# An attention and expert kernel: first expert weights asked for later, unread matmuls in free banks, transfers counted for each queue

## The chip, the core and the metric

The kernel runs on one core of one Trainium2 chip. The core has five engines that each run their own list of instructions in order: TensorE (PE, matrix multiplies, with its weight loads shown apart as PEld), VectorE (DVE), ScalarE (ACT), GpSimd (POOL) and SyncE (SP, which here only issues DMA transfers). They wait for each other through semaphores. The metric is the time of one execution in microseconds (us), taken on the device.

## The reference

The input is attention over 8 batches of 8 heads, 576 positions, 64 wide; the first four heads see a window of the last 32 positions, the other four every fourth of the last 128. Its output, 4608 rows of 512, goes through a layer of eight experts, of which each row takes the one with the highest logit:

```python
scores = scale * np.matmul(q, k.transpose(0, 1, 3, 2))
...
scores = np.where(masks[None, :, :, :], scores, -1000000000.0)
...
attn = attn / (np.sum(attn, axis=-1, keepdims=True) + 1e-09)
return np.matmul(attn, v).astype(np.float32)
...
logits = x @ w_gate
expert_idx = np.argmax(logits, axis=1)
...
for e in range(E):
    lo, hi = (boundaries[e], boundaries[e + 1])
    h = np.maximum(x_sorted[lo:hi] @ w1[e], 0.0)
    y_sorted[lo:hi] = h @ w2[e]
y = y_sorted[inv_perm]
return (gate_w[:, None] * y).astype(np.float32)
```

Everything is fp32: w1 is 512 x 1024 and w2 1024 x 512 for each expert, 2 MB each.

## The kernel before

**The stages.** Attention is cut into 16 pairs (a batch and one of the two kinds of heads), each in two units. A unit goes: `scores` on PE (L602), mask on DVE (L618), exp on ACT (L636), sums and reciprocals on DVE, scaling on POOL (L653), transposes of the scaled weights on PE into a bank called `weights` (L664), their eviction from that bank by ACT or DVE (`eT`, L894), and the product with `v` on PE (`xo`, L692). After both pairs of a batch are done, PE computes the gate's logits and the ranks of the rows within their experts, POOL scatters the rows of that batch into a table in DRAM (`bucket`), and tables say which expert owns which 128 rows.

The experts' work has four parts. Eight single slots of 128 rows run between the attention units as soon as a batch fills them (`ph`, L1525, is the first product, `py`, L1541, the second); the weights of the first two are asked for early, as eight transfers of 1 MB (L522). Then come ten pairs of slots: two slots' products share fourteen smaller ones, for which DVE adds up blocks of the two experts' weights and rows (L1819), PE multiplies (L1925 and L1932), and DVE puts the results together (L2055). Between the pairs run fourteen blocks of 32 rows (`ph_s`, L1635, and `py_s`) for what is left of an expert. Five slots close the kernel. Results are scattered to the output by POOL (L1566).

**What sets the order.** Nothing of this order is written out by hand. Each step is given to `Plan` with an estimated duration, a rank, the buffers that it takes and uses and the steps that it comes after (`after`). `Plan.write` then plays the kernel through with these estimates: it keeps the time at which each engine is free, picks the step that could start soonest, of those within 0.25 us the one with the lowest rank, and writes it out. Each engine then executes its steps in the order written. An `after` that no data and no buffer stands behind is thus only a place in the order; in the kernel itself there is no wait for it. For transfers the plan keeps a time until which the DMA engines move data (`moving`), to which each transfer adds its `moved`.

**Queues.** SP issues `q` and `k` (both into `raw`, L386), `v` (L412, L419, L436), the first weights (L522), the weights (L1511) and rows `x` (L1482) of single slots, the rows of 32-row blocks (`own`, L1588), and the pairs' rows `xp` (L1482) and weights (L1790, two buffers for w1 and two for w2, in turn). Each of SP's transfers also waits for the one eight places ahead of it. POOL issues the scatters and, on its own queue, the weights of 32-row blocks (L1623): w1 as two transfers into `raw`, w2 as one into `raw` and two into `qT`.

**Unread matmuls.** Where the plan sees PE idle, or its clock low, it writes small matmuls whose result nobody reads (L732), ahead of the step that PE would idle for. The plan's count is `max(min(MOST, int(idle / us)), WARMING if cold else 0)`. They write to the last quarter of the bank that `weights` or `rank` last took (`spare[0]`), so they come behind whatever still reads that bank. They end with the first matmul of the first single slot.

Of the kernel before, what the change touches and what calls it, by code (L numbers as in the profile page):

```python
# [33 lines left out]
CAP = N  # L34
# [15 lines left out]
NSLOT = SINGLES + max(E, MOST_SLOTS - FIRSTS - 2 * PAIRS)  # L50
TAIL = SINGLES + 5
# [22 lines left out]
MOVED_S = 1.5  # L74
# [47 lines left out]
class Plan:  # L122
# [19 lines left out]
    APART = 0.21 * IDLE  # L142

# [67 lines left out]
    def write(self):  # L211
# [8 lines left out]
        while open_:  # L220
# [114 lines left out]
def kernel(  # L335
# [222 lines left out]
    def turn_pe(p, n, m):  # L558

        tp = bank("turned", 6, 64)  # L560
# [99 lines left out]
    def weights(ev, g):  # L660
        tp = bank("weights", 4, 128)
        spare[0] = tp[:, 3]
# [61 lines left out]
    def hold(name):  # L724
        return Hold(ring[name])
# [3 lines left out]
    spare = [bank("unread", 4, 128)[:, 3]]  # L729

    def fill():
        nc.tensor.matmul(spare[0], lhsT=idle, rhs=idle, start=True, stop=True)  # L732
# [19 lines left out]
    def attention():  # L752
# [12 lines left out]
        for p, (b, ty) in enumerate(pairs):  # L765
# [40 lines left out]
            )  # L806
            hq, hk = hold("qT"), hold("kT")
            turned[p] = []
            for n in range(2 if p < BY_PE else 0):
                for m in range(3):  # L810
                    hb, T = hold("misc"), {}
# [27 lines left out]
            quad = p < QUADS  # L839
            for hp in range(2):  # L840
# [3 lines left out]
                if hp == 0 or not quad:  # L844
# [4 lines left out]
                    def score(e, i=i, units_of=units_of, tags=tags):  # L849
# [4 lines left out]
                        "PE", 1.76 if p < BY_PE else 3.35 if quad else 1.7 if p < WHOLE else 0.88, score,  # L854
# [76 lines left out]
    def route(b, hx, parts, other):  # L931
# [86 lines left out]
        def ranks():  # L1018
            rk = bank("rank")
            spare[0] = rk[:, 384:512]  # L1020
# [126 lines left out]
    table_done, slot_known, sent_all = [], {}, []  # L1147
# [317 lines left out]
    def fetch_x(j):  # L1465
# [9 lines left out]
        at0 = nc.sync.value_load(ints["basei"][:, n : n + 1], min_val=0, max_val=E * CAP)  # L1475
        rows_of(at0, x, gt, b)

    def rows_of(at0, x, gt, b):
        rows = bucket[ds(at0, 128), :].rearrange("(t i) f -> i t f", i=32)
        for g in range(4):  # L1480
            read_bucket(
                nc.sync.dma_start(  # L1482
# [4 lines left out]
        if gt is not None:  # L1487
# [3 lines left out]
            read_bucket(nc.sync.dma_start(gt, two), b)  # L1491
# [188 lines left out]
    def short_slots():  # L1680
# [6 lines left out]
        for i in range(SOME + 1):  # L1687
            j, D = ranked(i), {}
            if i < SOME:
# [5 lines left out]
                        after=[known, *in_turn["first"]],  # L1695
                        takes=[hw[n]], rank=890.0 + j + 0.4 + 0.7 * n, moved=MOVED_S / 2,
# [78 lines left out]
    def fetch_pair(u, t, D):  # L1775
# [6 lines left out]
        rows_of(at0, D["x", t], None if t else D["gt"], B - 1)  # L1782
# [18 lines left out]
    def pair_unit(u, last, rank0):  # L1801
# [46 lines left out]
        in_turn["ld"] = ld  # L1848

# [233 lines left out]
    def moe():  # L2083
# [6 lines left out]
        for i, s in enumerate(firsts):  # L2090
            s.after = [firsts[i - 1]] if i else []
# [199 lines left out]
```

## Time and profile before

| | |
|---|---|
| median of 3 runs | 748.86 us (744.45 to 752.41) |
| the profiled execution | 747.48 us, of which the span is 745.7 us |
| mean granted clock of PE over the span | 0.982 |
| data moved | 192.48 MB, 258 GB/s on average |

The lines quoted below come from the profile of that one execution. A line of a group gives the source line, the engine, the operation, what it writes and reads, shapes and the number of instructions; behind the first bar the busy time in us and the mean ns of one; behind the second the idle time of the engine just before these instructions, and what ended it. A line of a timeline begins with the start and the duration in us; an engine's name with a q (SPq) is its DMA queue's issuing; a bracket at the end gives the idle time ahead and what released it. "issue" means that the engine waited for nothing that the profile shows. An fp32 matmul leaves two matmul records.

### The profile page before, as it was taken

To read this page: it belongs to the slowest core of one execution; us is meant where nothing else is said; L and a number is where in the kernel's file an instruction comes from. 1 tells how busy PE (TensorE), PEld (TensorE's weight loads), DVE (VectorE), ACT (ScalarE), POOL (GpSimd) and SP (SyncE) were. 2 spreads that over 40 slices of the span, in tenths; PEclk is the share of its full clock that TensorE was granted. 3 is DMA by queue.
4 is the path that set the end of the run, shared out by engine and by line. 5 is a ranking of instruction groups with operands and counts; after the bars stand their busy time and mean duration, and the time that the engine had idled before them with its cause. 6 is when DMAs were issued, how large, how long until landed. Compare 5 with 4: busy or idle time off the path is not lost. (4 is left out here: it accounts for less than half of the span.)

```text
span 745.7 us, 21945 instructions
## 1 busy us (share of the span) xinstructions
PE 704.6 (94%) x8462; PEld 592.5 (79%) x8462; DVE 454.5 (61%) x1018; ACT 275.1 (37%) x895; POOL 213.9 (29%) x551
## 2 busy tenths in 40 slices
PE   5869989999999999999789999999999999999996
PEld 5857887867877878677578898998998989997674
DVE  6957886767765875372348858668587585840000
ACT  1756856565655687411112121221212212111111
POOL 1213433413424445263011233033131232412011
PEclk9889999999999999999989999999999999999999
DMA  9897976798999899699789497577787679979850
GB/s 263 275 288 229 259 243 166 223 269 246 282 244 298 244 277 250 256 335 326 283 268 305 146 362 238 186 280 261 240 292 257 207 247 386 294 244 336 294 194 31
DMA packets 139073, 192.48 MB, mean 258 GB/s; under 512 B 67884, under 2 KB 87086, under 8 KB 138448
## 3 DMA queue, kind: packets, MB, share of 16 engines
q1 hardware_dynamic: 124832, 145.36, 63.7%
q0 software_dynamic: 12976, 44.86, 16.3%
q8 instruction: 69, 1.13, 0.6%
q10 hardware_dynamic: 1152, 0.76, 0.4%
q14 instruction: 44, 0.36, 0.1%
HBM read 209.01 MB, written 20.22 MB: 307 GB/s over the span
## 5 line engine op out<-in xcount | busy, mean ns | idle before, releaser
L636 ACT ACTIVATE e<-e,lo 128x96 f32<-128x96 f32 x288 | 103.7, 365 | 22.7 <-DVE lo L630 22.5
L1566 POOL DMA_INDIRECT out_dram<-y,to x33 | 40.2, 1217 | 221.0 <-DVE to L2076 118.7
L1525 PEld LDWEIGHTS ph<-xt,w 128*128 128x128 f32 x832 | 96.5, 192 | 5.0 <-issue 4.0
L1525 PE MATMUL ph<-xt,w 128*128 128x128 f32 x832 | 99.8, 276 | 0.2 <-issue 0.2
L1541 PE MATMUL py<-w,h 128*128 128x512 f32 x208 | 94.6, 595 | 0.0
L653 POOL TENSOR_TENSOR e<-e,rec 128x864 f32<-128x864 f32 x32 | 52.3, 1634 | 127.8 <-DVE rec L649 92.9
L602 PE MATMUL scores<-kT,qT 32*64 32x96 f32 (+1 forms) x2160 | 56.7, 260 | 10.8 <-issue 4.4
L1541 PEld LDWEIGHTS py<-w,h 128*128 128x128 f32 x208 | 37.3, 190 | 37.0 <-issue 36.9
L602 PEld LDWEIGHTS scores<-kT,qT 32*64 32x64 f32 (+1 forms) x2160 | 49.3, 140 | 17.8 <-issue 15.1
L500 POOL DMA_INDIRECT bucket<-rows,idx x40 | 39.1, 978 | 57.6 <-issue 15.7
L636 ACT ACTIVATION_READ_ACCUMULATOR e<-e,lo 128x1 f32 x288 | 54.9, 191 | 0.0
L618 DVE SCALAR_TENSOR_TENSOR e<-scores,cst 128x384 f32<-128x384 f32 (+1 forms) x128 | 45.5, 394 | 13.8 <-PE scores L602 9.6
L692 PE MATMUL xo<-eT,v 96*64 96x64 f32 (+1 forms) x1280 | 45.8, 225 | 4.0 <-issue 3.5
L692 PEld LDWEIGHTS xo<-eT,v 96*64 96x64 f32 x1280 | 40.7, 138 | 10.6 <-issue 6.9
L894 ACT COPY eT<-weights 96x384 f32<-96x384 f32 x89 | 40.4, 481 | 19.9 <-PE weights L664 15.9
L664 PE MATMUL weights<-cst,e 128*96 128x128 f32 x288 | 45.9, 287 | 1.7 <-DVE eT L894 0.7
L664 PEld LDWEIGHTS weights<-cst,e 128*96 128x96 f32 x288 | 31.7, 133 | 12.7 <-issue 5.8
L1925 PEld LDWEIGHTS Z<-xt,w 128*128 128x128 f32 x320 | 37.4, 192 | 3.8 <-issue 3.4
L740 POOL MEMSET still<- 128x1 f32 x343 | 35.2, 103 | 17.0
L1925 PE MATMUL Z<-xt,w 128*128 128x128 f32 x320 | 39.8, 278 | 0.0
L1517 DVE STREAM_TRANSPOSE xt<-x 128x512 f32<-128x512 f32 x13 | 9.1, 706 | 49.7 <-PE ph L1525 36.6
L1932 PE MATMUL Z<-w,h 128*128 128x256 f32 x160 | 38.6, 384 | 0.0
(248 smaller groups left out, 1271.8 us busy)
## 6 DMA issues: line engine op xcount, KB each, us to landing
w<-in_moe_w_dram SPq DMA_DIRECT2D x46, 2048.0 KB
raw<-in_moe_w_dram POOLq DMA_DIRECT2D x42, 1024.0 KB
qT<-in_moe_w_dram POOLq DMA_DIRECT2D x28, 512.0 KB
w<-in_moe_w_dram SPq DMA_DIRECT2D x8, 1024.0 KB
raw<-in_q_dram SPq DMA_DIRECT2D x14, 576.0 KB
raw<-in_k_dram SPq DMA_DIRECT2D x14, 576.0 KB
v<-in_v_dram SPq DMA_DIRECT2D x7, 864.0 KB
xp<-bucket SPq DMA_DIRECT2D x80, 64.0 KB
```

The lines of the kernel that those rows point to most:

```text
L500: nc.gpsimd.indirect_dma_start(out=bucket, out_offset=bass.IndirectOffsetOnAxis(ap=idx, axis=0), in_=rows, in_offset=None, bounds_check=NR ...
L602: nc.tensor.matmul(two[r][QB * half : QB * half + QB, KB * c : KB * c + KB], lhsT=qT[:, QB * n : QB * n + QB], rhs=kt[:, QB * n : QB * n + ...
L618: nc.vector.scalar_tensor_tensor(out=e[p, c0 : c0 + w], in0=sc[r][p, a : a + w], scalar=-SCALE, in1=m[p, a : a + w], op0=OP.mult, op1=OP.add,)
L636: nc.scalar.activation(out=ev[:, c], in_=ev[:, c], func=AF.Exp, bias=lo[:, c : c + 1], scale=-1.0, accum_out=den[:, c : c + 1],)
L653: nc.gpsimd.tensor_tensor(out=ev, in0=ev, in1=rec.unsqueeze(2).broadcast_to([128, NC, KB]), op=OP.mult)
L664: nc.tensor.transpose(tp[0:KB, c], ev[:, 3 * g + c], ident)
L692: nc.tensor.matmul(xo[DH * r : DH * r + DH, g, lo - half_s * g : hi - half_s * g], lhsT=v0[:, hd, n] if ty == 0 else v1[:, n, hd], rhs=eT[ ...
L894: copier(e)(S_["eT"][:, 3 * g : 3 * g + 3], S_["w", g][0:KB, 0:3])
L1525: nc.tensor.matmul(ph[:, f % 4], lhsT=w1s[home(j)][:, c, 128 * f : 128 * f + 128], rhs=xt[:, c], start=c == 0, stop=c == 3,)
L1541: nc.tensor.matmul(py, lhsT=h[:, f], rhs=w2s[home(j)][:, f], start=f == 0, stop=f == 7)
L1566: i = nc.gpsimd.indirect_dma_start(out=out, out_offset=bass.IndirectOffsetOnAxis(ap=to, axis=0), in_=y, in_offset=None, bounds_check=out.s ...
L1925: nc.tensor.matmul(to[:, f], lhsT=right[:, c, 128 * f : 128 * f + 128], rhs=left[:, c], start=not more and f == c == 0, stop=c == 1, skip_ ...
```

## The change

The change has five parts.

1. The first two single slots' weights (L522): in the plan they came after nothing; now the first of them comes after the `v` of the third pair.
2. Unread matmuls: before each group, the plan looks through four rings of banks (`slot`, `s`, `two`, `misc`) for one whose oldest bank it has seen come free and which the step itself does not need. There the group goes, up to four together as one matmul of 512 columns. If there is none, there is no group.
3. The plan's `moving` is kept for SP, ACT and POOL apart, and a transfer that begins while another queue moves takes 1.6 times as long in the plan.
4. Weights of the 32-row blocks: in the plan they come after the first pair's weights where they came after the first pair's rows; the `moved` of each of their two steps is 5.2 for the first block and 2.0 for the others, where it was 0.75 for all.
5. Code for another order of transposes and for rows fetched by POOL (`BY_PE`, `BY_POOL`). Both constants are 0, and nothing of it is in the program.

```diff
-MOVED_S = 1.5
+MOVED_S = 4.0
...
+    SHARED = 1.6
...
-        self.moving = start
+        self.moving = dict.fromkeys(("SP", "ACT", "POOL"), start)
...
+    def unread(self, s, at):
+        for ring in self.unread_in:
+            old = ring.free_at()
+            if old is None or self.seen(old, "PE") > self.free["PE"]:
+                continue
+            h = Hold(ring)
+            h.end = self.free["PE"]
+            ring.holds.append(h)
+            needs = [t.ring.free_at() for t in s.takes]
+            if None not in needs and max((self.seen(n, "PE") for n in needs), default=0.0) <= at:
+                return h
+            ring.holds.pop()
+        return None
...
-                for _ in range(max(min(self.MOST, int(idle / us)), self.WARMING if cold else 0)):
-                    self.fill()
-                    self.free[e] = self.matmuls(self.free[e], self.FILL, self.FILL)
+                count = max(min(self.MOST, int(idle / us)), self.WARMING if cold else 0)
+                unread = self.unread(s, max(at, self.free[e] + count * us)) if count else None
+                if unread:
+                    self.fill(unread.ring, count)
...
-                    self.moving = max(self.moving, t + 0.65 * self.LANDS) + s.moved / s.dmas
-                    lanes.append(self.moving + 0.35 * self.LANDS)
+                    begin = max(self.moving[e], t + 0.65 * self.LANDS)
+                    shared = any(q != e and m > begin for q, m in self.moving.items())
+                    self.moving[e] = begin + s.moved / s.dmas * (self.SHARED if shared else 1.0)
+                    lanes.append(self.moving[e] + 0.35 * self.LANDS)
...
-    def fill():
-        nc.tensor.matmul(spare[0], lhsT=idle, rhs=idle, start=True, stop=True)
+    def fill(of, count):
+        (name,) = [n for n, r in ring.items() if r is of]
+        to = two_banks("unread")[:, 0] if name == "two" else bank("unread", tag=name)
+        for n in [4] * (count // 4) + [count % 4] * (count % 4 > 0):
+            nc.tensor.matmul(
+                to[:, 0 : 128 * n].rearrange("p (n x) -> p n x", n=n), lhsT=idle,
+                rhs=idle.unsqueeze(1).broadcast_to([128, n, 128]), start=True, stop=True,
+                skip_group_check=True,
+            )
...
-                        after=[known, *in_turn["first"]],
-                        takes=[hw[n]], rank=890.0 + j + 0.4 + 0.7 * n, moved=MOVED_S / 2,
+                        after=[known, *in_turn["first_w"]],
+                        takes=[hw[n]], rank=890.0 + j + 0.4 + 0.7 * n, moved=MOVED_S / 2 if i else 5.2,
...
-            s.after = [firsts[i - 1]] if i else []
+            s.after = [firsts[i - 1]] if i else [loaded[2]]
```

The lines of the program move with the change: L732 becomes L756, L602 L625, L664 L686, L692 L714, L618 L641, L386 L409, L412 L435, L436 L459, L522 L545, L1482 L1513, L1525 L1556, L1541 L1572, L1566 L1597, L1623 L1654, L1790 L1821, L1819 L1850, L1925 L1957, L1932 L1964 and L2055 L2087.

**SP, from the sixth `q` on.** The names are buffers: `raw` takes `q` and `k`, `v_71` and `v_72` take `v` of the two kinds of heads, `w_0_90` and `w_0_92` are the first expert's w1 and w2. Before:

```order
L386 DMA raw<-in_q_dram 128x1152
L386 DMA raw<-in_k_dram 128x1152
L522 DMA w_0_90<-in_moe_w_dram 128x2x1024
L386 DMA raw<-in_q_dram 128x1152
L386 DMA raw<-in_k_dram 128x1152
L522 DMA w_0_90<-in_moe_w_dram 128x2x1024
L412 DMA v_71<-in_v_dram 96x36x64
L386 DMA raw<-in_q_dram 128x1152
L386 DMA raw<-in_k_dram 128x1152
L522 DMA w_0_92<-in_moe_w_dram 128x4x512
```

The same stretch of SP with the change:

```order
L409 DMA raw<-in_q_dram 128x1152
L409 DMA raw<-in_k_dram 128x1152
L409 DMA raw<-in_q_dram 128x1152
L409 DMA raw<-in_k_dram 128x1152
L435 DMA v_71<-in_v_dram 96x36x64
L409 DMA raw<-in_q_dram 128x1152
L409 DMA raw<-in_k_dram 128x1152
L545 DMA w_0_90<-in_moe_w_dram 128x2x1024
```

The first two transfers of weights stand behind the `v` (L435) and the `q` and `k` that they were ahead of; the third, `w_0_92`, comes later than this stretch.

**PE, from the third group of unread matmuls on.** `weights` are the transposes that are evicted to `eT`. Before:

```order
L732 MATMUL unread<-idle 128x128 x3
L664 MATMUL weights<-cst,e 96x128 x9
L732 MATMUL weights<-idle 128x128 x3
L692 MATMUL xo<-eT,v_71 64x64 x8
L692 MATMUL xo<-eT,v_71 64x32 x4
L692 MATMUL xo<-eT,v_71 64x64 x8
L664 MATMUL weights<-cst,e 96x128 x6
L732 MATMUL weights<-idle 128x128 x7
```

With the change:

```order
L756 MATMUL unread<-idle 128x256
L686 MATMUL weights<-cst,e 96x128 x9
L756 MATMUL unread<-idle 128x384
L714 MATMUL xo<-eT,v_71 64x64 x8
L714 MATMUL xo<-eT,v_71 64x32 x4
L714 MATMUL xo<-eT,v_71 64x64 x8
L686 MATMUL weights<-cst,e 96x128 x6
L756 MATMUL unread<-idle 128x512
L756 MATMUL unread<-idle 128x384
```

The groups stand in the same places and have nearly the same width, but each is one or two instructions, and they write to a bank of their own (`unread`). In the whole program 135 unread matmuls of 128 columns become 43 of up to 512, 131 times 128 columns together.

**PE, from the last rank step to the first pair.** `w_0_90` and `w_1_91` are w1 of two slots in turn, `w_0_92` and `w_1_93` w2. Before:

```order
L1026 MATMUL rank<-oh,cst 128x40
L1541 MATMUL py<-w_0_92,h 128x512 x4
L1525 MATMUL ph<-xt,w_1_91 128x128 x32
L1541 MATMUL py<-w_1_93,h 128x512 x8
L1525 MATMUL ph<-xt,w_0_90 128x128 x32
```

With the change:

```order
L1056 MATMUL rank<-oh,cst 128x40
L1556 MATMUL ph<-xt,w_0_90 128x128 x4
L1572 MATMUL py<-w_0_92,h 128x512 x8
L1556 MATMUL ph<-xt,w_1_91 128x128 x32
L1572 MATMUL py<-w_1_93,h 128x512 x8
L1556 MATMUL ph<-xt,w_0_90 128x128 x32
```

Four `ph` and four `py` that stood ahead of the rank step now stand behind it; what follows up to the pair is the same in both. On POOL the first 32-row block's five transfers stood together between the scatters of slots 6 and 7; now its two of w1 stand there and the three of w2 behind the scatter of slot 7. On SP, near the first pair, slot 7's w2 (L1542) stands behind the first four rows of `xp` instead of ahead of them, and the pair's w2 behind eight `own` instead of four.

More of the change, by code (lines that the diff above doesn't have):

```diff
@@ L50 @@
 NSLOT = SINGLES + max(E, MOST_SLOTS - FIRSTS - 2 * PAIRS)
+BY_POOL = 0
 TAIL = SINGLES + 5
@@ L233, in write @@
                 us = self.FILL * self.slowed(self.free[e])
-                for _ in range(max(min(self.MOST, int(idle / us)), self.WARMING if cold else 0)):
-                    self.fill()
-                    self.free[e] = self.matmuls(self.free[e], self.FILL, self.FILL)
+                count = max(min(self.MOST, int(idle / us)), self.WARMING if cold else 0)
+                unread = self.unread(s, max(at, self.free[e] + count * us)) if count else None
+                if unread:
+                    self.fill(unread.ring, count)
+                    for _ in range(count):
+                        self.free[e] = self.matmuls(self.free[e], self.FILL, self.FILL)
+                    unread.end, unread.on = self.free[e], e
             if e == "PE":
@@ L558, in turn_pe @@
     def turn_pe(p, n, m):
-        tp = bank("turned", 6, 64)
+        tp = bank("turned", 6, 64, tag="slot")
         for c in range(6):
@@ L728 @@
     nc.gpsimd.memset(idle, 1.0)
-    spare = [bank("unread", 4, 128)[:, 3]]
-    def fill():
-        nc.tensor.matmul(spare[0], lhsT=idle, rhs=idle, start=True, stop=True)
+    def fill(of, count):
[7 more added lines that the diff above has]
+            )
+    plan.unread_in = [ring[name] for name in ("slot", "s", "two", "misc")]
     plan.fill = fill
@@ L810, in attention @@
                 for m in range(3):
-                    hb, T = hold("misc"), {}
+                    hb, T = hold("slot"), {}
                     one = add(
@@ L1474, in fetch_x, with rows_of @@
         xs[j], gts[j] = x, gt
-        at0 = nc.sync.value_load(ints["basei"][:, n : n + 1], min_val=0, max_val=E * CAP)
-        rows_of(at0, x, gt, b)
-    def rows_of(at0, x, gt, b):
+        queue = nc.gpsimd if j < BY_POOL else nc.sync
+        at0 = queue.value_load(ints["basei"][:, n : n + 1], min_val=0, max_val=E * CAP)
+        rows_of(queue, at0, x, gt, b)
+    def rows_of(queue, at0, x, gt, b):
         rows = bucket[ds(at0, 128), :].rearrange("(t i) f -> i t f", i=32)
@@ L1481, in rows_of @@
             read_bucket(
-                nc.sync.dma_start(
+                queue.dma_start(
                     x[32 * g : 32 * g + 32], rows[:, :, PART * g : PART * g + 128]
@@ L1490, in rows_of @@
                 two = two.rearrange("(t i) f -> i t f", i=128)
-            read_bucket(nc.sync.dma_start(gt, two), b)
+            read_bucket(queue.dma_start(gt, two), b)
     whose = {}
@@ L1781, in fetch_pair @@
         )
-        rows_of(at0, D["x", t], None if t else D["gt"], B - 1)
+        rows_of(nc.sync, at0, D["x", t], None if t else D["gt"], B - 1)
     def fetch_pair_w(u, n, D):
@@ L2100, in ask @@
             hx = hold("x")
-            asked[j] = (
-                add("SP", 3.5, lambda e: fetch_x(j), after=[known, *sent],
-                    takes=[hx], rank=900.0 + j, moved=1.4, dmas=5),
-                hx,
-            )
+            if j < BY_POOL:
+                get = add("POOL", 4.6, lambda e: fetch_x(j), after=[known, *sent], takes=[hx],
+                          rank=120.0 + j, moved=1.4, dmas=5, plain=True)
+            else:
+                get = add("SP", 3.5, lambda e: fetch_x(j), after=[known, *sent], takes=[hx],
+                          rank=900.0 + j, moved=1.4, dmas=5)
+            asked[j] = get, hx
         for j in range(3):
```

10 lines of the change are left out of this document (5 added, 5 removed).

## The prediction

> **What bounds the kernel now.** I read the page's head first, then the busy time in stretches of 20 us, then what TensorE (PE) waited for, then the timelines of PE, SyncE (SP) and GpSimd (POOL) at those waits.
>
> ```profile
> span 745.7 us, 21945 instructions
> PE 704.6 (94%) x8462; PEld 592.5 (79%) x8462; DVE 454.5 (61%) x1018; ACT 275.1 (37%) x895; POOL 213.9 (29%) x551
> q8 instruction: 69, 1.13, 0.6%
> ```
>
> PE is busy for 94% of the span: of the whole, only what makes PE idle or slow can pay. The third row is a queue that carries instructions, 69 packets; it comes back below.
>
> The next fence holds, for a stretch of time, the busy us and instruction count of PE, PE's weight load, VectorE (DVE), ScalarE (ACT) and POOL, then PE's granted clock, the DMA share and GB/s.
>
> ```profile
> 20.00:40.00 20.00, 17.08 (x421) 15.33 (x420) 18.88 (x38) 12.86 (x61) 6.52 (x4) 0.84 0.90 285
> 40.00:60.00 20.00, 15.18 (x290) 12.67 (x287) 10.07 (x20) 12.56 (x50) 3.27 (x2) 0.83 0.94 235
> 340.00:360.00 20.00, 20.00 (x108) 13.78 (x107) 7.90 (x12) 2.57 (x4) 4.67 (x6) 1.00 0.95 335
> 360.00:400.00 40.00, 30.86 (x219) 27.67 (x218) 21.22 (x34) 6.33 (x12) 5.14 (x12) 0.91 0.81 274
> 400.00:720.00 320.00, 320.00 (x3101) 279.54 (x3101) 187.90 (x309) 64.55 (x127) 75.69 (x203) 1.00 0.79 269
> ```
>
> From 400 to 720 us (the last row) PE is saturated, so what the change does there can't give time and costs some only if it breaks that. Two places have room: the stretch from 20 to 60 us, with PE at 17.08 and 15.18 of 20 and a clock of 0.84 and 0.83, and 360 to 400 us, where 9.1 us are missing. The waits of PE up to 400 us say what ended them (us in total, times, longest):
>
> ```profile
> PE A L1925 <- DVE h L1819: 6.7, 1, 6.7
> PE scores L602 <- issue: 4.4, 4, 3.7
> PE xo L692 <- issue: 3.5, 3, 2.0
> PE scores L602 <- DVE e L618: 3.2, 4, 1.6
> PE weights L732 <- ACT eT L894: 2.3, 4, 0.6
> ```
>
> The largest single wait of the kernel after its start is the first row: PE stands 6.7 us before a product of the first pair of expert slots. The two "issue" rows are 7.9 us in which PE waited for nothing that the profile shows.
>
> **The first pair's stall.** All engines around it, in order of time:
>
> ```profile
> 358.21 1.95 PE L1925 MATMUL Z<-xt,w 128*128 128x128 f32 x16
> ...
> 368.52 1.23 DVE L1819 TENSOR_TENSOR v<-w 128x1024 f32<-128x1024 f32 x1 [11.22 <-DMA w<-in_moe_w_dram]
> ...
> 374.00 3.78 PE L1925 MATMUL A<-xt,w 128*128 128x128 f32 x16 [6.69 <-DVE h L1819]
> ...
> 389.71 0.71 DVE L1852 STREAM_TRANSPOSE xt<-xp 128x512 f32<-128x512 f32 x1 [3.61 <-DMA xp<-bucket]
> ...
> 392.46 1.99 PE L1932 MATMUL A<-w,kT 128*128 128x256 f32 x8 [2.45 <-DVE y L2055]
> ```
>
> The pair starts at 358.21. Two experts' sums of weights (DVE L1819) can't begin until the pair's second weights have landed, at 368.52, after 11.22 us of waiting; some sums later PE gets its operand at 374.00. The matmuls behind the gap ran at the lower clock, 3.78 us where the same sixteen took 1.95. So this place costs 6.69 + (3.78 - 1.95) = 8.5 us. PE was ready at 374.00 - 6.69 = 367.31; the landing would have had to be at 368.52 - 6.69 = 361.8, 3.6 us after the pair's start, and was 10.3 after it. At the pair's end PE waits 2.45 us more for a sum (DVE L2055) that stands on DVE behind a transpose, which waited 3.61 us for rows of `xp`. Why the weights are late, on SP and then on POOL:
>
> ```profile
> 341.30 0.39 SPq L1790 DMA_DIRECT2D w<-in_moe_w_dram  x1
> ...
> 349.97 0.39 SPq L1790 DMA_DIRECT2D w<-in_moe_w_dram  x1
> ```
>
> ```profile
> 347.96 0.77 POOL L1623 DMA_DIRECT2D raw<-in_moe_w_dram  x1 [1.62 <-issue]
> ...
> 350.57 1.46 POOL L1623 DMA_DIRECT2D qT<-in_moe_w_dram  x2
> ```
>
> ```profile
> w<-in_moe_w_dram SPq DMA_DIRECT2D x46, 2048.0 KB
> raw<-in_moe_w_dram POOLq DMA_DIRECT2D x42, 1024.0 KB
> qT<-in_moe_w_dram POOLq DMA_DIRECT2D x28, 512.0 KB
> ```
>
> The first pair's w1 (2.1 MB) is asked for at 341.30, its w2 only at 349.97, since each SP DMA waits for the one eight places ahead of it, and there that chain leads to w1. Between them, from 347.96 on, POOL puts the whole of the first 32-row block's weights on its own queue, 2 + 2 pieces, 1.0 + 1.0 + 1.0 (`raw`) and 0.5 + 0.5 (`qT`), 4.2 MB. So 8.4 MB go in from 341.30 to 368.52, 27.2 us, which is 309 GB/s; the window from 340 us shows the engines nearly full at 335 GB/s (share 0.95).
>
> What changes: POOL's plan cost for these weights is larger, and their steps follow the pair's own weights in the plan. In the order that comes out, w1 of the short block still goes out first; only w2 (2.1 MB) moves, to behind the next scatter, which belongs to slot 7 and ends about when the pair starts. There is no wait in hardware on the pair's loads. On SP the pair's w1 and w2 keep their places after each other, but slot 7's w2 (2.1 MB) now sits behind the first `xp`, just ahead of the pair's w1. So up to the landing of the pair's w2 the bytes are again 2.1 (slot 7's) + 2.1 + 2.1 (POOL) + 2.1 = 8.4 MB. What is gained is the start, which hangs on the tables of the last batch. PE's order has 4 `ph` and 4 `py` more between the last rank step and the pair than before. Their price, and the first and last `ph`:
>
> ```profile
> L1525 PE MATMUL ph<-xt,w 128*128 128x128 f32 x832 | 99.8, 276 | 0.2 <-issue 0.2
> L1541 PE MATMUL py<-w,h 128*128 128x512 f32 x208 | 94.6, 595 | 0.0
> ```
>
> ```profile
> L1525 PE MATMUL ph<-xt,w x832: 269/275/377, 142.9 to 732.4; 128*128 128x128 f32 x167
> ```
>
> A fp32 matmul is two records, so a `ph` is 99.8/416 = 0.24 us, a `py` 94.6/104 = 0.91: 4.6 us more of PE work hide the transfers. By the old pace w2 then lands 10.3 - 4.6 = 5.7 us after the pair's start, at 335 GB/s (25.1 us instead of 27.2) at 3.6. It has to be there at 3.6: a stall of 0 to 2.1 us (2.5 should the pace fall a little), taken as 1.0, and too short to lower the clock as the 6.69 did. Gain 8.5 - 1.0 = 7.5.
>
> The second stall I leave as it is. The `xp` rows that it waits for stand behind the second pair's weights; these start with w2's landing, so earlier, but the 2.1 MB that POOL now sends at the pair's start run beside them. At 309 GB/s these are 6.8 us. Bounds: 2.45 gained to 4 lost (6.8 less some of the earlier start). Sum for the place: **-7.5**, with ends -8.5 - 2.45 = -11 and -6 + 4 = -2.
>
> The Trainium skill (DMA: Bandwidth & Descriptors, § Queues, rings and completion order) says that each DMA engine takes turns between the queues that have work, a packet at a time. By that rule POOL's 2.1 MB, as long as they move, take up to half the engines from the pair's w2, so halving them cannot do more than halve that loss, and the other half is put on the second pair's weights. The trace agrees in its sum (w2 alone needs 2.1 MB over 18.5 us, 113 GB/s, while all queues did 335).
>
> **The early weights.** Eight transfers of 1 MB, the first two singles' weights, move back on SP behind the third pair's `v`.
>
> ```profile
> 39.48 0.68 PE L692 MATMUL xo<-eT,v 96*64 96x64 f32 x13 [1.97 <-issue]
> 50.33 2.55 PE L602 MATMUL scores<-kT,qT 32*64 32x96 f32 x94 [3.67 <-issue]
> 56.73 0.85 PE L692 MATMUL xo<-eT,v 96*64 96x32 f32 x21 [1.13 <-issue]
> ```
>
> ```profile
> 29.46 0.51 SPq L522 DMA_DIRECT2D w<-in_moe_w_dram  x1
> ```
>
> The first of them goes out at 29.46, the second behind one more `q` and `k`; `v` of the third pair, with the `q` and `k` behind it, is now ahead of both. PE stops three times here for "issue", 1.97 + 3.67 + 1.13 = 6.8 us, while the DMA share is 0.90 and 0.94 and, by the page, instructions come over a DMA queue as well: I read these stops as PE out of instructions, waiting behind 2 MB of weights that no `ph` uses before 142 us (the row of `ph` above). The clock goes to 0.84 and 0.83 in these windows, at most 0.16 x 20 + 0.17 x 20 = 6.6 us of PE work. Nothing else waits for the moved bytes: `q`, `k` and `v` were early already and gain no time on PE. But the `v` and `q`, `k` that come ahead fill the same queue 10 us later, so the second and third stop can remain. I count the first stop and half of its slow clock, 1.97 + 1 = **-3**; ends 0 and -9 (all stops, a third of the clock). The last of the eight is passed by one `q`, `k` and the `v` pieces of a pair, which moves it by a few us against a first `ph` at 142.8: cost 0.
>
> The Trainium skill (Runtime: NRT & Kernel Launch, § Instruction fetch mechanics) says that an engine fetches its next block of instructions by itself while it runs the current one, and that the crossing is mostly hidden. By that the moved bytes give nothing here, and the sum is 3 us higher; the three stops of 1 to 4 us in this trace do not look hidden, but no row names the fetch as their cause.
>
> **The unread matmuls.** These keep PE's clock up in gaps that the plan foresees.
>
> ```profile
> L732 PE MATMUL weights<-idle 128*128 128x128 f32 x204 | 28.8, 283 | 3.0 <-ACT eT L894 2.3 <-DVE eT L894 0.7
> ```
>
> Before, each wrote to the bank of the newest `weights` or `rank` tile and had to wait for its eviction: 3.0 us, and 0.3 at `rank`. Now each goes to a bank that the plan sees free, and up to four are one of 512 columns. 102 + 27 + 6 = 135 of 128 columns become 131 times 128 in 43 instructions. Four single ones are 4 x 28.8/102 = 1.13 us, one wide one, 128 x 512 like a `py`, 0.91. If all lay on PE's path: 28.8 x (1 - 0.91/1.13) = 5.6 us and 3.3 us of waits. But a fill that runs in a real gap costs nothing either way, and a step behind it then waits for the same eviction itself. I take 2 of the waits and 1.5 of the width: **-3.5**; ends -9 and, if the new bank is not free in fact, a loss (below). The shift of the `moving` count to one per queue and the later steps of the other short blocks only reorder: after 400 us PE is full although each block moves 4.2 MB, so that cover hides it: cost 0, and 1 or 2 us where a block's weights came late.
>
> **Sum.** -7.5 - 3 - 3.5 = -14 from the profiled execution of 747.48 us gives **733.5**. That execution is 1.4 below the median of 748.86.
>
> **The rivals.** (1) *The start gives nothing*: the stops for "issue" only move, and the fills lie in real gaps. For it: beside the stops PE's waits up to 400 us are few and short, so most of the stretch runs at the pace of PE's own order. Against it: the stops themselves, which stand right behind the first weights. 747.5 - 7.5 = 740. (2) *The pair's stall only moves*: the same 8.4 MB, and the second stall grows by 4. For it: the count of bytes above; against it: 4.6 us more of cover. 747.5 - 2 - 6.5 = 739. This is also the case in which the change doesn't do what it says, for "later" is only a place in POOL's order, and half of the bytes don't move at all. Both together: 745.5. (3) *Slower: the free banks are not free.* The new banks are those that `scores` use too, so a fill can wait for DVE's masks, and a late mask then stops PE at each of 43. For it: PE does wait for masks at `scores`, 3.2 us in 4 waits. If each fill waited 0.58 us, as the four behind an eviction did (2.3/4), that is 25 us: 747.5 + 25 - 7.5 - 3 = 762. It decides from 10.5/43 = 0.24 us a fill on. Against it: DVE is busy for 61% only and those waits are four in all.
>
> **Chances.** Forecast 0.50 (its own range 727 to 737), rival 1 0.17, rival 2 0.15, both 0.09, rival 3 0.09. About 1% is what a measurement of this kernel can tell, so faster means under 741.4 and slower over 756.3. Faster: 0.50 and most of rivals 1 and 2 (0.14 + 0.12) make 0.76; slower: 0.09; the rest is 0.15. The range goes up to "both" (745.5) and down to 733.5 less 6 for the stops (their end of -9) and 4 for the second stall and the fills: 723 to 746.
>
> **What would show it.** Right: the wait of L1957 (L1925 before) on DVE's h under 2.5 us and its sixteen matmuls near 1.95; the landing of the pair's w2 within 2 to 6 us of the pair's start; "issue" waits of PE below 6 us up to 60 us; the fills' own wait under 1 us; PE at 20.00 of 20 from then to the end. Wrong: a new wait of PE at the end of the first pair or at the first `ph_s`; fills that wait for DVE L641; the same 6.8 us of issue in other places; or any window with PE under 20.00 late.

## The result

The change makes the kernel 1.2% slower: 757.74 us (median of 4 runs, 756.47 to 760.58) against 748.48 us before (4 runs), a ratio of 1.0121 with a 95% interval of 1.0076 to 1.0165. The forecast was 733.5 us, with 723 to 746 as its range. Executions of a kernel fall into a faster and a slower state, and a ratio is formed from runs in the faster one alone, so it is not just the quotient of the two medians. The profiled execution has a span of 754.7 us, 9.0 more than before. The page, and then the busy time in stretches (the columns as in the prediction):

```profile
span 754.7 us, 21591 instructions
PE 705.8 (94%) x8278; PEld 576.4 (76%) x8278; DVE 457.4 (61%) x1015; ACT 275.2 (36%) x898; POOL 215.2 (29%) x572
```

```profile
20.00:40.00 20.00, 18.40 (x426) 13.97 (x428) 19.00 (x37) 15.18 (x68) 6.52 (x4) 0.88 0.80 244
40.00:60.00 20.00, 17.18 (x359) 12.92 (x355) 16.24 (x36) 17.12 (x77) 4.90 (x3) 1.00 0.77 206
160.00:180.00 20.00, 10.79 (x105) 10.27 (x106) 7.78 (x16) 5.56 (x23) 1.63 (x1) 0.62 0.68 191
260.00:280.00 20.00, 15.32 (x205) 12.95 (x206) 11.76 (x21) 12.61 (x55) 7.58 (x12) 0.93 1.03 236
400.00:720.00 320.00, 318.57 (x3104) 278.64 (x3105) 195.95 (x326) 63.66 (x126) 76.73 (x199) 1.00 0.79 270
```

PE has idle time in new places. From 20 to 60 us it is busier than before (18.40 and 17.18 us against 17.08 and 15.18). From 160 to 180 us it works for 10.79 of 20 us at a clock of 0.62. These are the same two windows before, in which PE stood less, 1.8 and 0.1 of 20 us, at a clock of 0.91 and 1.00:

```profile
160.00:180.00 20.00, 18.22 (x288) 12.46 (x289) 13.87 (x30) 13.46 (x55) 5.90 (x4) 0.91 0.86 239
260.00:280.00 20.00, 19.93 (x315) 14.96 (x314) 15.03 (x27) 16.01 (x68) 8.66 (x14) 1.00 0.91 271
```

What PE waited for up to 420 us says where the time goes (us in total, times, longest):

```profile
PE scores L625 <- DVE e L641: 11.5, 4, 9.6
PE weights L686 <- POOL e L676: 4.7, 1, 4.7
...
PE scores L625 <- issue: 3.7, 3, 2.4
PE A L1957 <- DVE h L1850: 3.0, 1, 3.0
PE A L1964 <- DVE y L2087: 3.0, 1, 3.0
PE xo L714 <- issue: 2.5, 1, 2.5
...
PE weights L686 <- issue: 1.6, 1, 1.6
PE unread L756 <- issue: 1.5, 1, 1.5
```

The wait of 6.7 us at the first pair has shrunk to 3.0, as forecast. A wait of 9.6 us for a mask (VectorE, L641) and one of 4.7 us for GpSimd's scaling (L676) are new. Both come from one pattern. The first, in order of time across SyncE, VectorE and PE:

```profile
151.21 0.40 SPq L1542 DMA_DIRECT2D w<-in_moe_w_dram  x1
...
152.98 1.92 SPq L1513 DMA_DIRECT2D x<-bucket  x4
...
157.96 9.30 SPq L1513 DMA_DIRECT2D x<-bucket  x4
...
167.42 0.71 DVE L1548 STREAM_TRANSPOSE xt<-x 128x512 f32<-128x512 f32 x1 [12.34 <-DMA x<-bucket]
...
168.16 1.45 DVE L641 SCALAR_TENSOR_TENSOR e<-scores,cst 128x384 f32<-128x384 f32 x4
...
169.02 0.55 PE L625 MATMUL scores<-kT,qT 32*64 32x96 f32 x2 [9.57 <-DVE e L641]
```

PE waits for a mask. The mask only takes 1.45 us, but VectorE takes its steps in the order written, and ahead of the mask stands the transpose of the third single slot's rows (L1548), which waited 12.34 us for these rows. They were asked for at 152.98, behind 2.1 MB of weights (L1542, 151.21, the third slot's w1). From 151.0 to 167.4 us SyncE's queue moved 5.1 MB, and these rows are 0.3 of them. The transpose did not need to be there: PE's first use of it, that slot's first `ph`, starts at 227.06, 60 us later. The same place before:

```profile
154.72 9.22 SPq L1482 DMA_DIRECT2D x<-bucket  x4
...
165.85 0.71 DVE L1517 STREAM_TRANSPOSE xt<-x 128x512 f32<-128x512 f32 x1 [3.28 <-DMA x<-bucket]
...
166.93 0.40 SPq L1511 DMA_DIRECT2D w<-in_moe_w_dram  x1
...
167.43 0.34 PE L602 MATMUL scores<-kT,qT 32*64 32x96 f32 x2 [1.07 <-DVE e L618]
```

Before, the third slot's w1 went out behind the rows, at 166.93. Even so the rows came at nearly the same time, 165.85 against 167.42, and VectorE waited for them before too, for 3.28 us. PE then lost only 1.07 us, because it arrived there later. The first `ph`, a mark on the way, is at 142.9 before and at 134.2 now:

```profile
L1556 PE MATMUL ph<-xt,w x832: 272/275/580, 134.2 to 741.3; 128*128 128x128 f32 x167
```

So PE is 8.7 us ahead at the mark. At the mask it is still 6.9 ahead: it arrives at 169.02 - 9.57 = 159.45, before at 167.43 - 1.07 = 166.36. The rows come 1.6 us later, and 1.07 + 6.9 + 1.6 = 9.6 is the wait. What was gained ahead of this point is lost at it. The second place has the same form:

```profile
256.11 7.43 SPq L1513 DMA_DIRECT2D x<-bucket  x4
...
264.26 1.94 SPq L425 DMA_DIRECT2D raw<-in_k_dram  x4
...
273.06 2.23 DVE L563 STREAM_TRANSPOSE kT<-raw 128x1152 f32<-128x1152 f32 x1 [5.60 <-PE weights L686]
...
276.02 1.63 POOL L676 TENSOR_TENSOR e<-e,rec 128x864 f32<-128x864 f32 x1 [8.33 <-DVE rec L672]
...
277.70 1.52 PE L686 MATMUL weights<-cst,e 128*96 128x128 f32 x6 [4.67 <-POOL e L676]
```

Here SyncE stands 7.43 us before a slot's rows, and `k` of the last pair goes out behind them, at 264.26. VectorE waits 5.60 us at the transpose of that `k` (the releaser named had long been done; a run below names the transfer). Behind it stand the reciprocals that GpSimd's scaling needs, and PE needs the scaled weights.

The first pair, with the last weights asked for ahead of it and behind its start:

```profile
349.68 0.39 SPq L1542 DMA_DIRECT2D w<-in_moe_w_dram  x1
...
368.34 0.39 SPq L1821 DMA_DIRECT2D w<-in_moe_w_dram  x1
...
372.14 1.95 PE L1957 MATMUL Z<-xt,w 128*128 128x128 f32 x16
...
377.76 0.78 POOL L1654 DMA_DIRECT2D raw<-in_moe_w_dram  x1
...
378.85 1.23 DVE L1850 TENSOR_TENSOR v<-w 128x1024 f32<-128x1024 f32 x1 [2.96 <-DMA w<-in_moe_w_dram]
...
384.26 2.05 PE L1957 MATMUL A<-xt,w 128*128 128x128 f32 x16 [3.03 <-DVE h L1850]
...
400.30 0.71 DVE L1884 STREAM_TRANSPOSE xt<-xp 128x512 f32<-128x512 f32 x1 [4.64 <-DMA xp<-bucket]
...
401.43 1.99 PE L1964 MATMUL A<-w,kT 128*128 128x256 f32 x8 [2.96 <-DVE y L2087]
...
403.35 1.45 PEld L1666 LDWEIGHTS ph_s<-raw,own 128*32 128x32 f32 x32 [0.33 <-issue]
```

The pair starts at 372.14 us, 13.9 later than before. PE waits 3.03 us for the sum, whose weights come 6.7 us after the pair's start where they came 10.3 after it, and the sixteen matmuls behind the wait take 2.05 and not 3.78. The second stall is 2.96 where it was 2.45. From the pair's start to the first `ph_s` it is now 403.35 - 372.14 = 31.2 us, before 36.2 (358.21 to 394.38 in that trace), so that the pair gives 5 us back. From 400 to 720 us PE is busy for 318.57 of 320 us; the 1.43 us that are missing are the end of the second stall, at 401.43, and behind it PE is full as before.

The account to the end is then: 8.7 us ahead at the first `ph`, 13.9 behind at the first pair, so 22.6 lost between; 5 won back in the pair; 9 behind at the end. Between the two marks PE has the same work in both kernels. The row of before, then that of the change:

```profile
142.85:358.21 215.36, 212.37 (x2778) 166.11 (x2775) 137.44 (x401) 116.39 (x416) 85.27 (x229) 0.99 0.92 280
134.17:372.14 237.97, 220.33 (x2776) 173.20 (x2775) 141.12 (x404) 116.84 (x418) 85.81 (x254) 0.94 0.85 256
```

PE idles for 17.6 us there (237.97 - 220.33) where it idled for 3.0, and the same matmuls keep it busy for 8.0 us more, at a clock of 0.94 and not 0.99: 14.6 + 8.0 = 22.6.

### The profile page after: what moved, and what is told of

Same layout as the page of the kernel before. It is cut to its first block, busy times and chain, and to the rows that moved or that the text cites. A ratio compares the mean times of both kernels' runs of the same rounds, so it can differ in the third digit from the quotient of the medians.

```text
span 754.7 us, 21591 instructions
## 1 busy us (share of the span) xinstructions
PE 705.8 (94%) x8278; PEld 576.4 (76%) x8278; DVE 457.4 (61%) x1015; ACT 275.2 (36%) x898; POOL 215.2 (29%) x572
## 3 DMA queue, kind: packets, MB, share of 16 engines
q0 software_dynamic: 12976, 44.86, 16.3%
## 5 line engine op out<-in xcount | busy, mean ns | idle before, releaser
L1556 PEld LDWEIGHTS ph<-xt,w 128*128 128x128 f32 x832 | 97.9, 195 | 5.7 <-issue 5.3
L1597 POOL DMA_INDIRECT out_dram<-y,to x33 | 40.9, 1239 | 212.8 <-DVE to L2108 81.0
L1556 PE MATMUL ph<-xt,w 128*128 128x128 f32 x832 | 101.0, 280 | 0.0
L676 POOL TENSOR_TENSOR e<-e,rec 128x864 f32<-128x864 f32 x32 | 52.3, 1634 | 155.1 <-DVE rec L672 101.3
L1572 PE MATMUL py<-w,h 128*128 128x512 f32 x208 | 96.1, 600 | 0.0
L625 PE MATMUL scores<-kT,qT 32*64 32x96 f32 (+1 forms) x2160 | 57.2, 260 | 18.8 <-DVE e L641 11.5
L625 PEld LDWEIGHTS scores<-kT,qT 32*64 32x64 f32 (+1 forms) x2160 | 50.2, 141 | 29.2 <-issue 24.9
L1572 PEld LDWEIGHTS py<-w,h 128*128 128x128 f32 x208 | 37.3, 192 | 35.0 <-issue 34.4
L641 DVE SCALAR_TENSOR_TENSOR e<-scores,cst 128x384 f32<-128x384 f32 (+1 forms) x128 | 45.7, 395 | 12.0 <-PE scores L625 9.7
L714 PEld LDWEIGHTS xo<-eT,v 96*64 96x64 f32 x1280 | 41.3, 141 | 14.8 <-issue 6.4
L686 PE MATMUL weights<-cst,e 128*96 128x128 f32 x288 | 45.7, 285 | 7.0 <-POOL e L676 4.7
L714 PE MATMUL xo<-eT,v 96*64 96x64 f32 (+1 forms) x1280 | 45.9, 228 | 3.1 <-issue 2.5
L686 PEld LDWEIGHTS weights<-cst,e 128*96 128x96 f32 x288 | 31.4, 132 | 19.3 <-issue 7.1
L756 PE MATMUL unread<-idle 128*128 128x512 f32 (+3 forms) x86 | 38.0, 553 | 5.7 <-POOL idle L750 4.2
L770 POOL MEMSET still<- 128x1 f32 x364 | 37.2, 102 | 18.0
L1957 PEld LDWEIGHTS Z<-xt,w 128*128 128x128 f32 x320 | 37.9, 192 | 2.0 <-issue 1.3
L1957 PE MATMUL Z<-xt,w 128*128 128x128 f32 x320 | 39.3, 276 | 0.0
L1964 PE MATMUL Z<-w,h 128*128 128x256 f32 x160 | 38.5, 383 | 0.0
```

The source lines that it names most:

```text
L625: nc.tensor.matmul(two[r][QB * half : QB * half + QB, KB * c : KB * c + KB], lhsT=qT[:, QB * n : QB * n + QB], rhs=kt[:, QB * n : QB * n + ...
L641: nc.vector.scalar_tensor_tensor(out=e[p, c0 : c0 + w], in0=sc[r][p, a : a + w], scalar=-SCALE, in1=m[p, a : a + w], op0=OP.mult, op1=OP.add,)
L676: nc.gpsimd.tensor_tensor(out=ev, in0=ev, in1=rec.unsqueeze(2).broadcast_to([128, NC, KB]), op=OP.mult)
L686: nc.tensor.transpose(tp[0:KB, c], ev[:, 3 * g + c], ident)
L714: nc.tensor.matmul(xo[DH * r : DH * r + DH, g, lo - half_s * g : hi - half_s * g], lhsT=v0[:, hd, n] if ty == 0 else v1[:, n, hd], rhs=eT[ ...
L1556: nc.tensor.matmul(ph[:, f % 4], lhsT=w1s[home(j)][:, c, 128 * f : 128 * f + 128], rhs=xt[:, c], start=c == 0, stop=c == 3,)
```

## The experiments

Three theories were on trial. **M**: the count of transfers for each queue misleads the plan. **F**: the first weights, asked for later, get in the way of later rows. **O** (order): any change of the plan's times makes another order of the steps, in which some step at the head of a line waits for late data. Later **H** (head of the line) and **W** (wall) stand for what the late data mean: H, that only the place of a few steps is wrong; W, that transfers are too late for everything. Each ratio is to the kernel before, run on the same chip, with its 95% interval; between two variants I compare these ratios. A difference between two variants in us is one of medians from different chips; where the ratios give another figure, it stands beside it.

### The changed kernel with one part undone

Without part 3:

```diff
-        self.moving = dict.fromkeys(("SP", "ACT", "POOL"), start)
+        self.moving = start
...
-                    begin = max(self.moving[e], t + 0.65 * self.LANDS)
-                    shared = any(q != e and m > begin for q, m in self.moving.items())
-                    self.moving[e] = begin + s.moved / s.dmas * (self.SHARED if shared else 1.0)
-                    lanes.append(self.moving[e] + 0.35 * self.LANDS)
+                    self.moving = max(self.moving, t + 0.65 * self.LANDS) + s.moved / s.dmas
+                    lanes.append(self.moving + 0.35 * self.LANDS)
```

> The changed kernel with one transfer count for all queues again (part 3 undone). Theory M: the count for each queue makes the plan ask for single slots' weights ahead of rows that VectorE then stands waiting for; without it the 9.6 us wait of PE for a mask near 160 us and the 4.7 us wait near 273 us go, and the time falls to 740 to 746. Theory F: the later first weights push 8 MB into the stretch where the slots' rows are needed; then this kernel stays at 755 to 760. Theory O: both waits come from an order that any change of the plan's times can make; then some other wait of 5 to 10 us stands there, at 745 to 758.

Measured: 755.85 us, 1.0055 (1.0013 to 1.0096). Not back to 740 to 746, so M alone is out; the interval still touches that of the changed kernel. PE's wait for the mask near 160 us is 3.5 us and a new one of 3.0 us for evicted rows stands near 316 us. F and O both have this time in their ranges, but O's wait of 5 to 10 us is not there.

Without part 1:

```diff
-            s.after = [firsts[i - 1]] if i else [loaded[2]]
+            s.after = [firsts[i - 1]] if i else []
```

> The changed kernel with the first two slots' weights asked for as before (part 1 undone). Theory F: 740 to 746, the waits near 160 and 273 us gone. Theory M: they stay, 755 to 760, and the early stops for issue come back on top, up to 4 more. Theory O: a wait of 5 to 10 us somewhere, 745 to 760.

Measured: 743.91 us, 0.9921 (0.9888 to 0.9955). The time is what F expected, but the waits that F wanted gone are there, 4.6 us for a mask at 169.8 us and 1.7 at 272.7. F explains the time and not how it comes about. O is missed narrowly on both counts, 745 us at least and a wait of 5 to 10.

Without part 2 (the old `fill`, one matmul of 128 columns each into `spare[0]`):

```diff
-    def fill(of, count):
+    def fill():
+        nc.tensor.matmul(spare[0], lhsT=idle, rhs=idle, start=True, stop=True)
```

> The changed kernel with the old unread matmuls behind evictions, 128 columns each (part 2 undone). All theories hold the new ones for a gain early on: 2 to 6 us slower than the changed kernel if the rest of the order stays, so 758 to 764. If the early gain is what runs into the late rows (what PE gains before 160 us it waits there), the same time as the changed kernel, within 2 us.

Measured: 751.71 us, 1.0033 (1.0002 to 1.0064), so faster than the changed kernel, which no theory had expected. PE still waits for the mask at 168.9 us, for 6.0 us and not 9.6. In this company the new fills cost more than they gain.

Without part 4:

```diff
-MOVED_S = 4.0
+MOVED_S = 1.5
...
-                        after=[known, *in_turn["first_w"]],
-                        takes=[hw[n]], rank=890.0 + j + 0.4 + 0.7 * n, moved=MOVED_S / 2 if i else 5.2,
+                        after=[known, *in_turn["first"]],
+                        takes=[hw[n]], rank=890.0 + j + 0.4 + 0.7 * n, moved=MOVED_S / 2,
```

> The changed kernel with the 32-row blocks' weights planned as before (part 4 undone). Nothing before 330 us should differ; the first pair's stall should be back from 3.0 to 6.7 us with its slow clock: 3 to 6 us slower than the changed kernel. If the stall's shrinking came from the earlier tables instead, no change within 2 us.

Measured: 756.63 us, 1.0105 (1.0061 to 1.015), not to be told from the changed kernel. GpSimd's five transfers stood ahead of the pair again, with a scatter between them, yet the stall of 6.7 us did not come back; two shorter ones of 2.6 and 2.1 us stood at the pair's first products instead. From the time at which PE is ready for the pair to the first `ph_s` it is 34.0 us, 31.2 in the changed kernel. So the pair alone is 2.8 us slower without part 4, which the intervals of the whole time are too wide to show.

### The kernel before with one part alone

The edits are those of the diff, one part at a time.

> The kernel before with the transfers counted for each queue, and nothing else. Theory M: 5 to 14 us slower, with PE waiting for a mask behind rows of a slot. Theory F: within 3 us of before. Theory O: anything from 5 faster to 14 slower, but by waits of this one sort.

Measured: 755.16 us, 1.0066 (1.0031 to 1.0101), 5.9 us more than the kernel before by the medians: within M's 5 to 14, and not within F's 3. PE waits 5.6 us for a mask at 172.7 us, and 3.9 us at 272.7.

> The kernel before with the first two slots' weights behind the third pair's v, and nothing else. Theory F: 5 to 14 us slower. Theory M: 2 to 4 us faster, by the stops for issue in the first 60 us. Theory O: anything from 5 faster to 14 slower, by waits for late rows.

Measured: 756.31 us, 1.0078 (1.0039 to 1.0117), 7.0 us more by the medians: within F's 5 to 14. M's expectation, 2 to 4 us faster, fails. PE waits 3.6 us for a mask at 167.1 us, 2.1 us for "issue" at 193.9 and 3.1 us for evicted rows at 321.1.

> The kernel before with the unread matmuls in free banks, up to 512 columns wide, and nothing else. 2 to 6 us faster if the rest of the order stays and the waits behind evictions (3.3 us) and the narrow form cost what the prediction took; no change if the next wait takes it up.

Measured: 745.56 us, 0.9947 (0.9916 to 0.9978), so 749.3 x 0.0053 = 4.0 us faster. Here every engine's order up to the first pair, but for the fills themselves, is that of the kernel before, and the term of the forecast holds.

> The kernel before with the 32-row blocks' weights planned behind the first pair's weights and with their larger transfer times, and nothing else. Up to 330 us nothing differs. The first pair's stall of 6.7 us shrinks to 0 to 3, the second stays at 2 to 4: 3 to 8 us faster. If the order of POOL's transfers is not what makes the pair's weights late, within 2 us of before.

Measured: 749.02 us, 0.9984 (0.9944 to 1.0024): no difference, and not the 3 to 8 us expected. The order of every engine is that of the kernel before until the first pair, GpSimd's too: alone, part 4 moves nothing there, and the stall is whole.

```profile
PE A L1926 <- DVE h L1819: 7.0, 1, 7.0
```

So that run is a second profile of the same program up to the first pair, and shows how far one profile can be trusted: the first `ph` starts at 138.4 us in it and at 142.9 in the kernel before.

Parts 1 and 3 each cost some 0.7% alone, and each in its own order: with either of them VectorE waits 6.7 to 12.3 us for the rows near 165 us (3.28 before), and in most also for `q` or `k` near 270. So M and F each get the time of their own part alone right and deny that of the other's, and the wait for the rows is there with either part: neither is the one cause. O is left, but it is the widest of the three and so far only argued. If O is right, the loss must go when those few steps are moved and nothing else.

### Moving single steps

A step with a `lag` is written out that many steps of its engine later; the plan and all else stay.

```diff
-            s.emit(e)
+            if s.lag:
+                self.lagged.append([s.lag, e, s])
+            else:
+                s.emit(e)
+                for one in list(self.lagged):
+                    if one[1] == e:
+                        one[0] -= 1
+                        if not one[0]:
+                            self.lagged.remove(one)
+                            one[2].emit(e)
...
+            xt.lag = LAG_XT.get(j, 0)
```

First the transpose of the third slot's rows (`LAG_XT = {2: 12}`):

> The changed kernel in which one VectorE step alone is written later: the transpose of the third single slot's rows stands 12 VectorE steps behind its place (PE's first use of it is some 45 us further on); every other order is the same. Theory H (head of the line): VectorE, which takes its steps in order, stood 12.3 us behind these rows, and PE 9.6 us behind VectorE's mask. Then the wait near 160 us and its slow clock go, and the kernel is 9 to 14 us faster than the changed one, 744 to 749. Theory W (wall): whatever stands next needs transfers that are late as well (the q and k behind the rows on SyncE), so that a wait of like size comes back within 30 us, and the time falls by less than 4.

Measured: 751.31 us, 1.0016 (0.9983 to 1.0048), 6.4 us under the changed kernel (7.9 by the ratios). The wait near 160 us is gone and no other comes within 50 us, as H has it; but less than H's 9 to 14 arrives, because the wait for the scaling near 270 us grows from 4.7 to 9.3. PE runs ahead to the next late step. In this run the trace names the transfer:

```profile
268.76 2.22 DVE L573 STREAM_TRANSPOSE kT<-raw 128x1152 f32<-128x1152 f32 x1 [10.20 <-DMA raw<-in_k_dram]
...
273.41 1.51 PE L696 MATMUL weights<-cst,e 128*96 128x128 f32 x6 [9.29 <-POOL e L686]
```

Then the transpose of that `k` behind the reciprocals as well (`LAG_TURN = {(15, 1): 1}`):

> As the run before, and the last pair's k transpose stands one VectorE step later, behind a unit's reciprocals. Theory H: the 4.7 us wait of PE for GpSimd's scaling near 273 us goes too, 3 to 6 us more, 739 to 745, which would be near the forecast. Theory W: no more than 1 us.

Measured: 747.12 us, 0.9975 (0.994 to 1.001), 4.2 less again by the medians (the intervals overlap), what H expected of the step, though 2 us above its range for the time. The wait for the scaling is gone, but the next step that needs the same `k` is the last pair's scores, and with it a mask:

```profile
249.82 7.82 SPq L1526 DMA_DIRECT2D x<-bucket  x4
...
258.69 1.76 SPq L435 DMA_DIRECT2D raw<-in_k_dram  x4
...
266.39 2.22 DVE L573 STREAM_TRANSPOSE kT<-raw 128x1152 f32<-128x1152 f32 x1 [9.70 <-DMA raw<-in_k_dram]
...
269.21 0.58 PE L635 MATMUL scores<-kT,qT 64*64 64x96 f32 x2 [7.40 <-DVE e L651]
```

`k` goes out at 258.69, behind rows that hold SyncE for 7.82 us, and PE waits 7.40. Next, on SyncE alone, and in the changed kernel without the lags, the third slot's w1 behind that slot's rows:

> The changed kernel in which only SyncE's order differs: the third slot's w1 (2.1 MB) is asked for behind that slot's rows, not ahead of them. If the rows are late because of the bytes ahead of them on the same queue, they land some 5 us sooner, PE's wait of 9.6 us shrinks to 3 to 6 and the time falls by 4 to 8 us, to 750 to 754. If they are late because the scatter that writes them is, nothing moves (755 to 760).

Measured: 752.39 us, 1.0052 (1.002 to 1.0084), 5.3 less than the changed kernel; the wait near 160 us is 2.2 us. The intervals touch, but the wait itself has gone from 9.6 to 2.2. The rows were asked for at 148.66 and were there at 158.53, 9.9 us later, where it had been 14.4 us (152.98 to 167.42): they are late because of the weights ahead of them on the same queue.

> The changed kernel without its part 1 (first weights as before) and with the third slot's transpose 12 VectorE steps later. Theory H: its own wait of 4.6 us near 169 us goes: 3 to 7 us under the 743.9 measured without the delay, 737 to 741. Theory W: 743 to 745.

Measured: 744.91 us, 0.9951 (0.991 to 0.9992), against 0.9921 without the lag: no difference that can be told, though the wait at 169 us is gone. One of 3.9 us at 263 us, for `q` and `k` that came late, has taken its place: W in time, H in kind. Last, on SyncE, the last single slot's rows behind the last pair's `k` (`LAG_X = {7: 1}`), added to the two lags:

> The changed kernel with the third slot's transpose and the last pair's k transpose later on VectorE, as in the run before, and in addition the last single slot's rows asked for on SyncE behind the last pair's k, where they stood ahead of it for 7.8 us. Theory H: the 7.4 us that PE still waited near 269 us for this k, and the slow clock behind it (0.74 over 20 us), go: 6 to 9 us less than the 747.1 of the two steps alone, 738 to 741. The forecast's gain was then made and lost again behind rows. Theory W: the transfers as a whole are too late there; less than 3 us, 744 to 747.

Measured: 741.62 us, 0.9869 (0.9824 to 0.9915), 5.5 us less than with two lags (7.9 by the ratios) and 16.1 less than the changed kernel (18.9 by the ratios). H's 6 to 9 us less and 738 to 741 are met by the ratios and just missed by the medians; W's less than 3 fails. Its waits of PE from 130 to 300 us, and two windows:

```profile
PE xo L725 <- DMA v<-in_v_dram: 2.7, 1, 2.7
PE weights L697 <- ACT eT L939: 0.9, 3, 0.5
PE scores L636 <- issue: 0.7, 1, 0.7
```

```profile
160.00:180.00 20.00, 19.63 (x335) 17.89 (x331) 17.41 (x43) 13.82 (x52) 10.27 (x28) 1.00 0.79 210
260.00:280.00 20.00, 19.66 (x281) 16.82 (x280) 15.41 (x34) 16.60 (x67) 5.10 (x4) 1.00 0.91 225
```

Both stretches are full at the full clock. The longest wait left is 2.7 us, for `v`, at 218 us. This trace is of the slowest of the six executions, 746.34 us, and still has a slow stretch behind that wait: from 220 to 240 us the clock is 0.68.

> The changed kernel without its part 1, with the third slot's transpose later, and with the last single slot's rows asked for behind the last pair's v, q and k. Theory H: its wait of 3.9 us near 263 us and the slow clock behind it go: 4 to 6 us less than 744.9, 739 to 741. Theory W: 743 to 746.

Measured: 742.65 us, 0.9889 (0.9843 to 0.9936), 2.3 us less than before the last step (4.6 by the ratios), so on the edge of H's 4 to 6; waits of 1.4 and 2.1 us for "issue" stand in the stretch from 220 to 250 us.

So moving three steps, two on VectorE and one on SyncE, takes 16 us off the changed kernel, and with them moved it is 1.3% faster than the kernel before: this version beats both. Leaving out part 1 without any lag gives 0.9921, and the two intervals overlap, so which of these two ways is the better one can't be told.

## Why the prediction was wrong

**The step that failed** is the one that costed the order between the first `ph` and the first pair at nothing: "only reorder: after 400 us PE is full ... cost 0", and before it "Two places have room". The sum had terms for 20 to 60 and for 360 to 400 us and none for 140 to 360, where 22.6 us were lost. In the trace of before PE idles for only 3.0 of 215.4 us there, but that says nothing of how soon the other engines' data would be there for a PE that comes earlier: the rows of a slot came just in time, and the 3.28 us of VectorE's and 1.07 us of PE's wait in the trace of before said how near the limit was. The lags show it: with three steps moved, 16.1 us come back. ("each block moves 4.2 MB" is too much as well: these transfers carry a condition, and the page of before has 44.86 MB on GpSimd's queue in all, scatters included, where fourteen blocks of 4.2 would be 58.8.)

**The early gain as a term.** "-3" for the stops and "-3.5" for the fills were meant as gains at the end. They were gains up to the next place that waits for data. The fills alone are worth 4.0 us (the run with part 2 alone), as forecast; in the changed order, undoing them makes the kernel faster. The stops for "issue" in the first 60 us went from 6.8 to 3.5 us, but two new ones, 1.46 us at 82.36 and 2.53 at 112.58, came behind them: up to 130 us PE's waits for "issue" are 7.3 us before, 7.7 with the change and 7.1 with its part 1 undone. So the stops moved, and the moved bytes gave nothing that lasted to the first `ph`; the prediction had named this reading too, with the sum 3 us higher. (The run with part 4 alone, the same program as before up to the pair, has 5.1.) The 8.7 us at the first `ph` are not these stops; up to 4.5 of them can be the difference between two executions. What ends the stops was not measured.

**The weights' place.** "cost 0" for the eight first transfers was right for their own use and wrong for what it left out: with any change of part 1 the plan puts other transfers and steps in another order downstream.

**The first pair.** "-7.5" was the right mechanism and too large. The cover, PE's work that hides the loads, grew by 5.6 us where 4.6 was forecast: the pair starts 22.5 us after the first of the four loads that the prediction counts (349.68 to 372.14), before 16.9 (341.30 to 358.21). But the four took 29.2 us to land and not 25.1 to 27.2, so the weights came 6.7 us after the pair's start, not 3.6 to 5.7, and the stall was 3.0 and not 1.0. The second stall was left as it was and is (2.96 against 2.45). Together 5.0 us, within the ends given.

The count of bytes left out how much the place of GpSimd's w2 is worth by itself. In the run with part 3 alone and in the one without part 1 (parts 2, 3 and 4) the pair starts at the same time, 366.88 and 366.70 us, its w2 goes out at 358.36 and 359.23, and the `ph` and `py` between the last rank step and the pair are the same. With part 3 alone GpSimd's five transfers go out together ahead of the pair, its w2 lands 10.2 us after the start and PE stalls for 6.69. Without part 1 three of the five go out behind the start, from 374.88, w2 lands 4.6 after it and PE stalls for 1.08. Part 4 alone changes no order there; it is worth something only in company.

**The rivals.** Rival 1 (the start gives nothing) had the stops right, which only moved, and the fills wrong. Rival 2 (the pair's stall only moves) did not come: the second stall grew by 0.5 us. Rival 3 had the right sign and the right instruction, a late mask, but the wrong reason: the fills wait for no mask, and the mask was late because of rows ahead of it on VectorE. No rival followed VectorE's and SyncE's order from one to the next.

## What to carry to other kernels

When a scheduler writes the order, an edit of its estimates is an edit of every engine's order, and PE being full in a stretch is no cover for it: go through the steps that wait for transfers, in the order of each engine, and ask what stands behind them. A step that waits for data and that nobody needs soon belongs behind the steps that others wait for; here moving three such steps was worth 16 us. Time gained early is kept only if nothing later is bound by data, so look for the next wait that the faster engine will run into before it is counted.

## What the runs showed of the hardware

Two executions of programs with the same order up to the first pair differ by 4.5 us at the first `ph` (142.9 and 138.4 us), more than half of it in stops for "issue" in the first 60 us (6.8 and 4.3 us). So here a single profile can't tell an early gain below that.

The waits cost more than their length. In the window of the 9.57 us wait, 160 to 180 us, the granted clock is 0.62 where it was 0.91 before, and the sixteen matmuls of the first pair took 3.78 us after 6.69 us of idling and 2.05 after 3.03.
